# One more product on TensorE in bias steps 1 to 20 of an attention and mixture-of-experts kernel

## The chip, the core and the metric

The kernel runs on one core of one Trainium2 chip. The time is the device time of one execution in microseconds (us). The median of three runs of the kernel before is 584.39 us (584.32 to 586.5).

## What is computed

The reference does attention over 4 batches, 8 heads, 576 positions and a head size of 64, and then a top-1 mixture of 8 experts on its output. The part that matters here is the position bias that is added to the scores:

```python
psi_rel = np.log1p(np.abs(rel))
psi_i = np.log1p(np.maximum(pos[:, None].astype(np.float32), 1.0))
x = (psi_rel / psi_i)[..., None]
h = np.maximum(x @ w1 + b1, 0.0)      # hidden size 32
bias = h @ w2                         # one value for each head
scores = scores + bias.transpose(2, 0, 1)[None, :, :, :]
```

The bias is the same for all batches. Softmax, the product with v, the gate and the experts follow.

## The kernel before, in words

**Bias.** The bias of 576 rows is made in 36 steps of 16 rows (`bias_step`, `emit_hid`, `emit_bias`); a step takes 4 groups of 4 rows. For each group a hidden layer `hd` (128 partitions: 4 rows by 32 hidden units; up to 576 distances) is made from the table of log distances `tab` at line 196 on VectorE, or for the fourth group of some steps at line 194 on ScalarE. Eight such tiles exist. At line 210 TensorE multiplies each with the second-layer weights `w2blk` (32 columns) in fp32; the four products go to the partitions 0, 32, 64 and 96 of one PSUM tile `sps`, so each uses a strip of 32 of the array's 128 columns. An fp32 product shows as two matmuls in the trace. Steps have 304 to 576 distances; over 512 they need a second, narrow product. ScalarE moves the tile out in two pieces (lines 216 and 217, the first mirrored) and SyncE's queue writes it to memory (`bias_d`, line 219). After every eighth step a block of 128 rows is read back from memory in the layout of the scores (`load_bias`, lines 165 to 167).

**Numbering.** In the loop, `kk_done[0]` counts the steps. Iteration c makes the hidden layers of the c-th step and the products of the one before, so the products made in iteration 1 are those of the first 16 rows that are done; the text calls them step 1. Steps 1 to 16 have 448, 432, ... 304, 304, ... 384 distances, steps 17 to 21 have 576, 560, 544, 528 and 512. The first eleven iterations run ahead of the attention, the next eight two to each of the first four score units, then one to each unit.

**Scores.** A score unit (`emit_s`) puts two f16 matmuls into each half of a `sps` tile of the same pool: there are two such tiles, shared by score units and bias steps. VectorE adds the bias and takes the maximum (line 325), ScalarE the exponential (line 330). Transposes (lines 389, 405), their eviction (395, 406) and the product with v (417, 420) follow some units later. The first four score units need the first block of the bias, the next four the second.

**Order.** Up to the last score unit a planner orders the instructions of each engine by their place in the program and its own estimate of when each can run (only SyncE's queue follows the program's order in part of it); the order is fixed before the kernel starts. Loading and splitting of q, k and v for the first batches (lines 124, 147, 150) share the engines with the first bias steps.

Of the kernel before, what the change touches and what calls it, by code (L numbers as in the profile page):

```python
# [48 lines left out]
def build(tc, nc, io):  # L49
# [6 lines left out]
    def load_pack(name, fields):  # L56
        t = const.tile(list(io[name].shape), F32, name="c_" + name)
        nc.sync.dma_start(out=t, in_=io[name])
        views, o = [], 0
        for w in fields:  # L60
            views.append(t[:, o:o + w])
            o += w
        return views
# [32 lines left out]
    w1c, b1c, psi, ri8, w2blk = load_pack("cpa", CPA)  # L96
    tab = tab_p.tile([128, S], F32, name="tab")
# [84 lines left out]
    on128 = const.tile([128, 1], F32, name="on128")  # L182
    nc.vector.memset(on128, 1.0)

    def reach(kk):
        return max(16 * kk + 16, S - 16 * kk)

    def emit_hid(kk):
        n = reach(kk)
        for ct in range(4):  # L190
            k = 4 * kk + ct
            hd = hid_p.tile([128, S], F32, name="hd")
            if ct == 3 and kk_done[0] in HACT:
                nc.scalar.activation(out=hd[:, 0:n], in_=tab[:, 0:n], func=AF.Relu, bias=bp[:, k:k + 1])
            else:
                nc.vector.tensor_scalar(  # L196
                    out=hd[:, 0:n], in0=tab[:, 0:n], scalar1=bp[:, k:k + 1], scalar2=0.0,
                    op0=ALU.add, op1=ALU.max,
                )
            hid_t[k] = hd  # L200

    def emit_bias(kk):
        n = reach(kk)
        nb, nf = 16 * kk + 15, S - 16 * kk
        ps = s_ps.tile([128, 2, 512], F32, name="sps").rearrange("p a j -> p (a j)")
        for c0, c1 in ((0, min(n, 512)), (512, n)):
            if c0 >= c1:
                continue
            for ct in range(4):
                nc.tensor.matmul(  # L210
                    out=ps[32 * ct:32 * ct + 32, c0:c1], lhsT=w2blk, rhs=hid_t[4 * kk + ct][:, c0:c1],
                    start=True, stop=True,
                )
        bv = bev_p.tile([128, S + 15], F32, name="bv")
        sc = ri8[:, kk:kk + 1]
        nc.scalar.activation(out=bv[:, 0:nb], in_=ps[:, nb:0:-1], func=AF.Copy, scale=sc)
        nc.scalar.activation(out=bv[:, nb:nb + nf], in_=ps[:, 0:nf], func=AF.Copy, scale=sc)
        o = 16 * kk * H * BP + BPAD - 15
        wr_t[kk] = nc.sync.dma_start(
            out=bias_d[o:o + 16 * (H * BP + 1)].rearrange("(i c) -> i c", c=H * BP + 1)[:, 0:H * BP]  # L220
            .rearrange("i (h p) -> i h p", p=BP)[:, :, 0:S + 15],
            in_=bv,
        )
# [3 lines left out]
    kk_done = [0]  # L227
# [3 lines left out]
    def bias_step(n):  # L231
        for _ in range(n):
            c = kk_done[0]
            if c > NKK:
                return
            if c < NKK:
                emit_hid(KORD[c])
            if c:
                emit_bias(KORD[c - 1])
                if c % 8 == 0 or c == NKK:  # L240
                    load_bias(0, KORD[c - 1] // 8)
                if c in PC[1:]:
                    load_pair(PC.index(c), 0)
                if c in VC:
                    load_v(VC.index(c), 0)
            kk_done[0] += 1
# [883 lines left out]
    out = io["out"]  # L1130
# [76 lines left out]
    with fin:  # L1207
# [18 lines left out]
        for i in range(2):  # L1226
            nc.tensor.matmul(
                out=cn[:, i:i + 1], lhsT=amat16[:, i], rhs=R["cs"][:, S - 1:S], start=True, stop=True
            )
        nc.vector.tensor_scalar(  # L1230
            out=nbc.rearrange("p a k -> p (a k)"), in0=bcut[0:32], scalar1=cn[:, 0:1], scalar2=None, op0=ALU.is_lt
# [7 lines left out]
        for i in (2, 3):  # L1239
            nc.tensor.matmul(out=cn[:, 2 + i:3 + i], lhsT=amat[:, i], rhs=nb[:, 2:3], start=True, stop=True)  # L1240
        nc.vector.scalar_tensor_tensor(
            out=R["thh"], in0=nb[:, 1:2], scalar=128.0, in1=cn[:, 1:2], op0=ALU.mult, op1=ALU.subtract
        )
        nc.vector.scalar_tensor_tensor(
            out=gp[:, 1], in0=cn[:, 1:2].to_broadcast([32, B]), scalar=-1.0, in1=gmat, op0=ALU.add, op1=ALU.mult
# [5 lines left out]
            out=rbox["h16"][:, 0:S], in0=R["cs"], scalar=R["thh"], in1=es, op0=ALU.is_gt, op1=ALU.mult  # L1251
# [3 lines left out]
            out=ecm[:, K1:NF], in0=c128[0:8, 0:NF - K1], scalar1=cn[0:8, 3:4], scalar2=None, op0=ALU.is_ge  # L1255
        )
        nc.vector.tensor_scalar(
            out=ecm[:, NF:], in0=c128[0:8, 0:NH], scalar1=cn[0:8, 5:6], scalar2=None, op0=ALU.is_ge
        )
        nc.vector.tensor_scalar(  # L1260
            out=hsh, in0=cn[:, 4:5], scalar1=cn[:, 3:4], scalar2=128.0 * (NF - K1), op0=ALU.subtract, op1=ALU.add
# [10 lines left out]
            out=ez, in0=ecm.unsqueeze(2).to_broadcast([8, NBLK, NE]),  # L1272
# [11 lines left out]
        for b in range(K1, K1 + 2):  # L1284
# [4 lines left out]
            out=mkp.rearrange("p k e -> p (k e)"), lhsT=on[0:8, 0:128], rhs=ez.rearrange("p k e -> p (k e)"),  # L1289
            start=True, stop=True,  # L1290
        )
        for b in range(K1, K1 + 2):
# [6 lines left out]
            out=mk, in0=mkp, in1=emadd.unsqueeze(1).to_broadcast([128, NBLK, NE]), op=ALU.add  # L1299
# [18 lines left out]
        for i, m in enumerate((FSURE, HSURE)):  # L1318
            nc.vector.tensor_scalar(
                out=rest[:, i:i + 1], in0=emp[:, NBLK + i:NBLK + i + 1], scalar1=-float(m), scalar2=0.0,  # L1320
# [5 lines left out]
            out=i1, in0=sls, scalar1=0.0, scalar2=float(NT // 2 - 1), op0=ALU.is_lt, op1=ALU.add  # L1326
# [5 lines left out]
            out=odh, in0=i1[:, NF:NF + HSURE], scalar1=2.0, scalar2=hmask[:, 1:2], op0=ALU.mult, op1=ALU.add  # L1332
# [155 lines left out]
```

## Time and profile before

| | |
|---|---|
| median of 3 runs | 584.39 us |
| the profiled execution | 583.0 us |
| its span, first to last instruction | 581.2 us |
| mean granted TensorE clock | 0.977 |
| TensorE matmuls busy | 536.6 us (92%) |
| VectorE busy | 469.1 us (81%) |
| ScalarE busy | 436.8 us (75%) |
| GpSimd busy | 262.4 us (45%) |

The times of instructions come from one profiled execution, counted from its first instruction. A granted clock of 1.00 is 2.4 GHz, 0.50 is 1.2 GHz. The clock is on record from about 8.4 us on; what is shown as 1.00 ahead of that has no record.

### The profile page before, as it was taken

Reading aid. Unit: us, or ns where it says so; the run is one execution under the profiler, and the core shown is the slowest. Engines: PE = TensorE matmul, PEld = TensorE weight load, DVE = VectorE, ACT = ScalarE, POOL = GpSimd, SP = SyncE. Lnnn points to the kernel's source line nnn. Section 1 sums busy time; section 2 is a strip of 40 time slices with the busy share of each in tenths; the row PEclk is TensorE's granted clock in tenths of the full one; section 3 lists DMA queues with packets and bytes.
Section 4 is the critical chain, followed back from the end, with each engine's and each line's share of the span. In section 5 each row is a group of like instructions: output and inputs, shape, how many; then the busy total and the mean of one; then the engine's idle time right before and its main releaser. Section 6 shows DMA issues by size and latency. Waiting matters only on the chain. (4 is left out here: it accounts for less than half of the span.)

```text
span 581.2 us, 14263 instructions
## 1 busy us (share of the span) xinstructions
PE 536.6 (92%) x5319; PEld 361.3 (62%) x5319; DVE 469.1 (81%) x913; ACT 436.8 (75%) x743; POOL 262.4 (45%) x293
## 2 busy tenths in 40 slices
PE   4777999989999999999999998999999999999992
PEld 1233445755666666767577777667776877777851
DVE  7977886688889989887977558869999799797960
ACT  5877887866988877877689965568898687886940
POOL 5100000795199968966744760642424264323121
PEclk9888999999999999999999997998999999999997
DMA  8765447755798799745175010597899957988250
GB/s 287 247 181 157 135 132 211 258 174 144 176 256 209 194 280 232 205 103 163 49 257 147 3 34 13 129 342 239 280 204 368 262 120 236 199 211 230 25 184 30
DMA packets 99613, 106.15 MB, mean 183 GB/s; under 512 B 66893, under 2 KB 76239, under 8 KB 95442
## 3 DMA queue, kind: packets, MB, share of 16 engines
q1 hardware_dynamic: 94752, 89.45, 55.4%
q0 software_dynamic: 4640, 15.43, 9.7%
q8 instruction: 44, 0.72, 0.5%
q10 hardware_dynamic: 146, 0.30, 0.1%
q14 instruction: 31, 0.25, 0.1%
HBM read 128.92 MB, written 20.80 MB: 258 GB/s over the span
## 5 line engine op out<-in xcount | busy, mean ns | idle before, releaser
L330 ACT ACTIVATE e<-e,st 128x576 f32<-128x576 f32 x144 | 111.6, 776 | 12.1 <-DVE st L325 10.8
L325 DVE CUSTOM_DVE_ANT_0 e<-sps,wb 128x576 f32<-128x576 f32 x144 | 106.8, 750 | 16.0 <-PE sps L306 8.8
L905 DVE TENSOR_TENSOR w<-wb,w 128x2048 bf16<-128x2048 f32 (+1 forms) x36 | 72.4, 2050 | 2.2 <-ACT w L898 1.9
L1002 POOL DMA_INDIRECT out_dram<-y,odx x17 | 31.7, 1865 | 90.3 <-ACT y L992 53.4
L305 PE MATMUL sps<-kh,qs 128*128 128x288 f16 x256 | 68.9, 290 | 3.4 <-DVE st L325 1.7
L389 PE MATMUL ta<-c_cpb,e 128*128 128x128 f32 x448 | 71.2, 280 | 0.5 <-ACT eT L395 0.2
L395 ACT COPY eT<-ta 128x512 f32<-128x512 f32 x96 | 54.9, 581 | 21.9 <-PE ta L389 20.5
L306 PE MATMUL sps<-kl,qs 128*128 128x288 f16 x256 | 68.2, 288 | 0.0
L898 ACT CAST w<-wb 128x2048 f16<-128x2048 f32 (+1 forms) x40 | 63.8, 1640 | 3.4 <-DMA wb<-in_w_dram 3.4
L937 PE MATMUL sps<-xT,we 128*128 128x128 f16 (+1 forms) x1056 | 62.9, 222 | 3.0 <-DVE we L905 1.7
L937 PEld LDWEIGHTS <-we 128*128 128x128 f16 (+1 forms) x1056 | 61.4, 99 | 6.5 <-DVE we L905 1.9
L976 PE MATMUL yp<-w,hhT 128*128 128x512 bf16 (+1 forms) x272 | 64.3, 379 | 0.0
L420 PE MATMUL av<-eT,vt 128*64 128x320 f32 (+1 forms) x384 | 62.4, 424 | 0.0
L210 PE MATMUL sps<-hd,c_cpa 128*32 128x512 f32 (+17 forms) x352 | 46.3, 520 | 16.7 <-DVE hd L196 10.3
L389 PEld LDWEIGHTS ta<-c_cpb,e 128*128 128x128 f32 x448 | 52.3, 142 | 12.8 <-issue 2.7
L196 DVE TENSOR_SCALAR hd<-tab,bp 128x448 f32<-128x448 f32 (+17 forms) x129 | 49.9, 446 | 4.9 <-PE sps L210 4.8
L905 DVE TENSOR_TENSOR we<-ws,we 128x2048 bf16<-128x2048 f32 (+1 forms) x25 | 49.0, 1992 | 4.6 <-ACT we L898 3.3
L937 PEld LDWEIGHTS <-wb 128*128 128x128 f16 (+1 forms) x1056 | 49.6, 101 | 2.8 <-issue 1.2
L937 PE MATMUL sps<-xT,wb 128*128 128x128 f16 (+3 forms) x1056 | 51.3, 212 | 0.0
L898 ACT CAST we<-ws 128x2048 f16<-128x2048 f32 (+1 forms) x26 | 41.4, 1636 | 4.1 <-DMA ws<-in_w_dram 4.1
L420 PEld LDWEIGHTS av<-eT,vt 128*64 128x64 f32 x384 | 26.9, 136 | 26.5 <-issue 8.2
L976 PEld LDWEIGHTS <-hhT 128*128 128x128 f16 x272 | 25.8, 98 | 28.4 <-issue 0.3
(234 smaller groups left out, 1012.1 us busy)
## 6 DMA issues: line engine op xcount, KB each, us to landing
ws<-in_w_dram SPq DMA_DIRECT2D x34, 1024.0 KB
wb<-in_w_dram SPq DMA_DIRECT2D x34, 1024.0 KB
hs<-in_w_dram SPq DMA_DIRECT2D x20, 1024.0 KB
bias_d<-bv SPq DMA_DIRECT2D x36, 295.5 KB
kf<-in_kt_dram SPq DMA_DIRECT2D x24, 288.0 KB
wb<-bias_d SPq DMA_DIRECT2D x16, 288.0 KB
wb<-bias_d SPq DMA_DIRECT2D x16, 256.0 KB
xrow_d<-xo SPq DMA_DIRECT2D x16, 256.0 KB
```

The costliest lines, as they stand in the source:

```text
L196: nc.vector.tensor_scalar(out=hd[:, 0:n], in0=tab[:, 0:n], scalar1=bp[:, k:k + 1], scalar2=0.0, op0=ALU.add, op1=ALU.max,)
L305: nc.tensor.matmul(out=ps[:, half, 0:288], lhsT=lq, rhs=kh[:, j], start=True, stop=False)
L306: nc.tensor.matmul(out=ps[:, half, 0:288], lhsT=lq, rhs=kl[:, j], start=False, stop=True)
L325: nc.vector.tensor_tensor_reduce(out=e, in0=ps[:, :, 0:288], in1=bsl, scale=-0.125, scalar=1e30, op0=ALU.add, op1=ALU.min, accum_out=st[:, ...
L330: nc.scalar.activation(out=e, in_=e, func=AF.Exp, scale=-1.0, bias=st[:, 0:1], accum_out=sm)
L389: nc.tensor.transpose(out=ta[:, j, :], in_=e[:, o:o + 128], identity=ident)
L395: nc.scalar.copy(out=eTv[:, :, hh, o:o + 128], in_=ta)
L420: nc.tensor.matmul(out=av[64 * x:64 * x + 64, 0:n], lhsT=vt[:, j, 64 * x:64 * x + 64], rhs=eT[:, 2 * j + x, 0:n], start=False, stop=(j == 3),)
L898: nc.scalar.copy(out=wh[c][:, sl], in_=src)
L905: nc.vector.tensor_tensor(out=wl[c][:, sl], in0=src, in1=wh[c][:, sl], op=ALU.subtract)
L937: nc.tensor.matmul(out=hp.rearrange("p a j -> p (a j)")[:, n * f:n * f + n], lhsT=w[f // 4][:, o:o + 128], rhs=x[:, kt], start=(i == 0), s ...
L976: nc.tensor.matmul(out=yp, lhsT=x[:, kt], rhs=w[kt // 4][:, 512 * (kt % 4):512 * (kt % 4) + 512], start=(i == 0), stop=(i == len(terms) - 1),)
```

## The change

In iterations 1 to 20 one more fp32 product is put ahead of the step's own. Its weights are the same `w2blk`, its columns the first 384 of `tab`, and it goes to partitions 0 to 31 of the step's own PSUM tile, where the first of the four products then starts anew and overwrites it.

```diff
+    KEEP = range(1, 21)
+
     def reach(kk):
         return max(16 * kk + 16, S - 16 * kk)
...
         ps = s_ps.tile([128, 2, 512], F32, name="sps").rearrange("p a j -> p (a j)")
+        if kk_done[0] in KEEP:
+            nc.tensor.matmul(out=ps[0:32, 0:384], lhsT=w2blk, rhs=tab[:, 0:384], start=True, stop=True)
         for c0, c1 in ((0, min(n, 512)), (512, n)):
```

## Rows read from the trace of the kernel before

**Rows 1.** The page: busy time and share; the granted clock in 40 slices.

```profile
PE 536.6 (92%) x5319; PEld 361.3 (62%) x5319; DVE 469.1 (81%) x913; ACT 436.8 (75%) x743; POOL 262.4 (45%) x293
PEclk9888999999999999999999997998999999999997
```

**Rows 2.** Stretches: length; busy us of PE, PEld, DVE, ACT, POOL; clock; DMA share, GB/s.

```profile
8.36:25.43 17.07, 10.44 (x50) 2.96 (x48) 16.49 (x38) 14.74 (x30) 5.94 (x13) 1.00 0.90 301
25.43:28.84 3.41, 3.27 (x16) 0.85 (x16) 2.87 (x6) 2.39 (x7) 0.00 (x0) 0.50 0.32 127
28.84:35.67 6.83, 3.65 (x25) 1.25 (x23) 4.65 (x13) 3.96 (x10) 0.00 (x0) 1.00 0.86 235
35.67:39.08 3.41, 3.23 (x16) 1.33 (x15) 2.58 (x10) 2.20 (x6) 0.00 (x0) 0.50 0.54 153
39.08:52.74 13.66, 10.18 (x104) 4.95 (x103) 11.60 (x31) 11.23 (x27) 0.00 (x0) 1.00 0.61 173
52.74:56.15 3.41, 3.41 (x23) 1.73 (x24) 1.98 (x5) 2.07 (x6) 0.00 (x0) 0.50 0.32 105
56.15:120.00 63.85, 62.92 (x506) 34.87 (x505) 46.44 (x128) 49.75 (x114) 14.37 (x25) 1.00 0.63 185
```

**Rows 3.** TensorE in order of time: start, us, instructions, wait before them.

```profile
14.10 1.26 PE L210 MATMUL sps<-hd,c_cpa 128*32 128x416 f32 x4 [1.82 <-DVE hd L196]
...
23.53 1.27 PE L210 MATMUL sps<-hd,c_cpa 128*32 128x336 f32 x6 [2.03 <-DVE hd L196]
25.57 4.11 PE L210 MATMUL sps<-hd,c_cpa 128*32 128x336 f32 x18 [0.77 <-ACT hd L194]
...
31.13 1.47 PE L210 MATMUL sps<-hd,c_cpa 128*32 128x304 f32 x8 [0.86 <-DVE hd L196]
34.04 0.75 PE L210 MATMUL sps<-hd,c_cpa 128*32 128x320 f32 x8 [1.44 <-ACT bv L217]
35.85 0.40 PE L305 MATMUL sps<-kh,qs 128*128 128x288 f16 x1 [1.06 <-DVE st L325]
...
51.33 0.28 PE L305 MATMUL sps<-kh,qs 128*128 128x288 f16 x1 [1.11 <-ACT bv L217]
...
56.98 1.06 PE L210 MATMUL sps<-hd,c_cpa 128*32 128x512 f32 x8
```

**Rows 4.** TensorE's waits from 5 to 57 us: us in total, times, longest.

```profile
PE sps L210 <- DVE hd L196: 10.3, 5, 5.2
PE sps L210 <- ACT bv L217: 2.7, 4, 1.4
```

**Rows 5.** TensorE in order of time: steps 14, 17 with 18, 19, and 20.

```profile
39.18 0.80 PE L210 MATMUL sps<-hd,c_cpa 128*32 128x352 f32 x8
...
45.38 2.12 PE L210 MATMUL sps<-hd,c_cpa 128*32 128x512 f32 x32 [0.81 <-ACT bv L217]
...
49.10 1.13 PE L210 MATMUL sps<-hd,c_cpa 128*32 128x512 f32 x16 [0.24 <-ACT bv L217]
...
52.74 2.02 PE L210 MATMUL sps<-hd,c_cpa 128*32 128x512 f32 x16 [0.76 <-DVE st L325]
```

**Rows 6.** ScalarE: evictions of steps 8 and 13; VectorE: the first score tile.

```profile
26.94 0.47 ACT L216 ACTIVATE bv<-sps,c_cpa 128x255 f32<-128x255 f32 x1 [0.86 <-PE sps L210]
38.39 0.54 ACT L216 ACTIVATE bv<-sps,c_cpa 128x335 f32<-128x335 f32 x1 [1.21 <-PE sps L210]
35.03 0.76 DVE L325 CUSTOM_DVE_ANT_0 e<-sps,wb 128x576 f32<-128x576 f32 x1 [1.08 <-DMA wb<-bias_d]
```

**Rows 7.** SyncE's queue: bias writes and loads; VectorE: the fifth score tile.

```profile
27.87 3.39 SPq L219 DMA_DIRECT2D bias_d<-bv  x3
31.48 0.41 SPq L165 DMA_DIRECT2D wb<-bias_d  x1
45.35 2.80 SPq L219 DMA_DIRECT2D bias_d<-bv  x2
51.92 0.76 DVE L325 CUSTOM_DVE_ANT_0 e<-sps,wb 128x576 f32<-128x576 f32 x1 [0.39 <-DMA wb<-bias_d]
```

## Prediction

> **What bounds the kernel now.** I read the page's shares first: TensorE is busy for 92% of the span, VectorE and ScalarE for 81% and 75% [rows 1]. So time that TensorE loses in a stretch where its own queue is full is lost for good, and time that it waits for others is not its to lose. The granted clock by slice shows where it ran below full speed. Then I cut the first 57 us at the edges of the clock's falls [rows 2]: from 25.43, 35.67 and 52.74 us the clock stands at 0.50 (1.2 GHz) for 3.41 us each, and in those three stretches TensorE is busy for 3.27, 3.23 and 3.41 us, while in the stretches between it is busy for only 10.44 of 17.07, 3.65 of 6.83 and 10.18 of 13.66 us. The clock falls where the queue is full again, after a thin stretch: ahead of the first fall stand waits of 2.03 and 0.77 us, ahead of the second 1.44 us (and another 1.06 before 35.85), ahead of the third 1.11 and 0.76 us [rows 3]. The waits tell what makes the thin stretches: hidden layers that VectorE or ScalarE has not yet made, and the two score tiles in PSUM that are not yet free ("bv L217" is their eviction) [rows 4]. From 56.15 to 120 us TensorE is busy for 62.92 of 63.85 us [rows 2]. So the reader should carry one number through: when the products of step 21, the first without an extra, start. Now it is 56.98 us [rows 3], and what is gained or lost there mostly reaches the end.
>
> **The change, part by part.** It removes nothing and moves nothing; no DMA, VectorE, ScalarE or GpSimd instruction is added. The constant KEEP issues nothing. Added are 20 fp32 products (each two matmuls with their weight loads), all on strip 0 of the array's columns (32 of 128).
>
> *Price of one extra.* Two steps of 576 and 560 columns, back to back at full clock, take 2.12 us; one of 544 takes 1.13 us [rows 5]. The second of the two thus adds 0.99 us for some 592 columns, 1.67 ns a column for a whole fp32 product of two passes. The extra has 384 columns: 384 x 1.67 = 0.64 us of strip 0. At half clock a step of 528 columns takes 2.02 us against 1.13 [rows 5], a factor of 1.8 to 2 a column, so 1.2 to 1.3 us. An extra is worth between nothing (its strip would have waited) and 1.3 us; all 20 exposed at full clock would be 12.8 us. Its weight loads have 32 columns like the products' own and cost nothing of their own while a matmul runs (the weight loader is the lesser of the two busy times in every stretch [rows 2]).
>
> *Whom it delays.* A step's four products go to four strips. Eight matmuls of 352 columns take 0.80 us [rows 5]; one after the other they would take 8 x 352 x 0.83 = 2.3 us, so strips run side by side. An extra therefore delays strip 0 of its step, and the step's end only where strip 0 is the last to finish. The Trainium skill says it otherwise ("TensorE: Matmul & The Clock Gate", Part 3, The mechanism: matmuls start and end in strict program order). With each product's two passes in program order that would hold strips 1 to 3 behind the extra too; the 0.80 us speak against it. By the rule step 11 would also pay its 0.64 us, and the sum below would be -0.6 instead of -1.2 us.
>
> *The wait it adds.* The extra needs the step's PSUM tile free; the step's first product waited for that as well. Behind it in TensorE's queue stand the step's four products and then scores and transposes.
>
> *Steps 1 to 11 (to 32 us): nothing.* Their tile is free before their last hidden layer is there. The rows show TensorE waiting on hidden layers at 14.10, 23.53, 25.57 and 31.13 us [rows 3], 10.3 us on VectorE's in all (5.2 of it ahead of the first product) [rows 4] and some more on ScalarE's. Strip 0, whose layer comes first, has the gaps to itself. If that cover were gone, 11 x 0.64 = 7 us.
>
> *First fall.* Extras of steps 8 and 9 lie in or beside the waits ahead of it (2.03, 0.77 us). If the clock holds, the eviction of step 8, which waited 0.86 us for TensorE until 26.94 [rows 6], starts some 0.6 us earlier (the last product's two passes of 336 columns, 2 x 0.56 at half clock against 2 x 0.28). That eviction matters: its write, issued at 27.87, lets the bias load go at 31.48, and the first score tile waits for that load until 35.03 [rows 6, 7]. So 0.6 us earlier there.
>
> *Steps 12 to 14 and the second fall.* Step 12 waits for its tile until 34.04, so its extra is exposed: 0.64 us. It falls on the eviction, and ScalarE later waits 1.21 us for TensorE (until 38.39) [rows 6], which takes it up. In the second fall 3.23 us of work shrink to 1.6; the extras of 13 and 14 put 1.3 back. Net -0.3, on top of the 0.6, less a little for coupling: I keep -0.6 us at 41 us.
>
> *Steps 15 to 18 (41 to 49 us): nothing.* All four are exposed on TensorE, 2.6 us, but the fifth score tile, which follows step 18 directly (the steps 17 and 18 end at 45.38 + 2.12 = 47.50 [rows 5]), is not evicted until 51.92, for want of its bias load [rows 7]. That load hangs on the write at 45.35 [rows 7]. So TensorE may be some 4 us late here; ScalarE, which sets the write, works without a wait in the meantime. Without that cover: 2.6 us.
>
> *Steps 19, 20 and the third fall.* Step 19's extra pushes its eviction and the next scores (51.33) by 0.64, of which the 0.6 us of the earlier load and the wait of 0.76 before 52.74 take back about half: step 20 starts 0.3 us early. The 3.41 us of work in the third fall need 1.7 at full clock, plus 0.64 for step 20's extra: 2.35 against 3.41, so -1.05. Together -1.35; step 21 waits for step 20's eviction, which does not shorten, so I take -1.2 us at step 21.
>
> *What is late next.* From there TensorE is the bound to 120 us [rows 2] and the same order of work follows 1.2 us earlier. Against the profiled execution (583.0 us, a span of 581.2 with 1.8 around it) that gives 581.8. That execution lies 1.4 us below the median of the timed runs, 584.39; the same -1.2 there gives **583.2 us**.
>
> The order is written by a planner that sees 20 more matmuls, and I cannot read from these rows what it then does with scores and transposes; I allow 2 us either way for that, three times one extra.
>
> **Rivals.**
> 1. *The clock falls all the same, and the extras are paid at half speed (slower).* For it: an extra fills 0.64 us of thin stretches whose waits sum to 2 to 3 us each [rows 3], and in two of them it waits for the same tile as the products, so it fills nothing until the tile comes. Against: a wait of 1.82 us before 14.10 did not bring the clock down [rows 2, 3], so waits about as long as these can pass. Place: step 13, in the second fall, at half clock costs 1.3 us, step 14 0.64; ScalarE's wait of 1.21 takes up the first part, so the write at 45.35 and the load behind it go 1.1 us later. Step 20 adds 1.3 at half clock. Sum +2.4 us: **586.8 us**. It decides from the second fall on: if 0.50 is still granted after 35 us, the sign turns. With steps 15 to 19 uncovered as well, +3.2: 590.
> 2. *The extras are all hidden, the clock holds (more gain).* Half of 3.27 + 3.23 + 3.41 = 5.0 us comes back, less only the extras of 13, 14 and 20 where these find another wait: -3 to -5, **580.4 us**. For it: waits of 10 us in the stretch. Against: from 33 us on the extra stands behind the same wait as the products.
> 3. *No change.* The clock holds but the score tiles go on waiting for bias loads whose time is set by VectorE's hidden layers and the DMA, and TensorE gets back in falls what it spends in extras: **584.4 us**. For it: the loads' round trips of 6.6 to 7.2 us [rows 7] have no TensorE in them.
>
> **How the numbers follow.** Chances: the forecast 0.40, rival 1 0.25, rival 2 0.13, rival 3 0.22. The forecast's own range is 581.2 to 585.2 (2 us either way for the planner). For 8 in 10 I reach to rival 2's 580.4 and to 587.8, past rival 1 by 1 us. A measurement of this kernel can tell some 0.5% (2.9 us) from no change: faster means under 581.5, slower over 587.3. Faster: nearly all of rival 2 and a fifth of the forecast (its low end), 0.20. Slower: some four tenths of rival 1, a tenth of the others for the planner, with steps 15 to 19 in it, 0.20. The rest, 0.60, is within.
>
> **What would show it.** Right: 1.00 granted from 9 to 120 us; the eviction of step 8 at about 26.3; the first score tile evicted at about 34.4, the fifth at 51.3; step 21 at about 55.8, with nothing changed behind it but the shift. Steps 1 to 11 wrong if VectorE shows waits on TensorE's products before 28 us. Wrong in the mechanism if 0.50 still stands after 35 or 52 us; wrong in the sum if step 21 moves and the end does not, or if matmuls, scores and transposes stand in another order on TensorE.

## The result, and the profile after

The changed kernel takes 589.45 us (median of 6 runs, 585.13 to 593.28), the kernel before on the same chip 583.27: a ratio of 1.0113 [1.0071, 1.0154]. On another chip it was 587.21 against 583.83, 1.0047 [1.0016, 1.0078]. The forecast was 583.2. The profiled execution of the changed kernel took 593.28 us, the longest of its six, against 583.0 for that of before; so its single times are read with care below, and the second profile of the changed kernel stands beside it where they differ. Line numbers behind line 205 are 4 higher than before: the extra is line 209, the products 214, the evictions 220 and 221, the score tile 329, the DMA transposes 354, the product that reads them 364.

The clock did what the forecast said. The page's first lines (answering to [rows 1]): no early slice is under 9 tenths.

```profile
PE 545.5 (92%) x5342; PEld 366.3 (62%) x5359; DVE 467.1 (79%) x913; ACT 437.6 (74%) x743; POOL 263.1 (44%) x293
PEclk9999999989989998999999997998999999999997
```

The stretches of [rows 2] in the changed kernel, and two later ones: 1.00 to 120 us. In the three stretches that ran at half clock before, TensorE is now busy for less of the time (2.51, 2.85 and 3.13 us against 3.27, 3.23 and 3.41), and from 56 to 120 us for as much as before. Behind 120 us it is busy for less of the time, at 0.94 and 0.97.

```profile
25.43:28.84 3.41, 2.51 (x20) 0.89 (x20) 3.04 (x7) 3.10 (x8) 0.00 (x0) 1.00 0.41 145
35.67:39.08 3.41, 2.85 (x22) 1.36 (x25) 1.84 (x8) 3.26 (x8) 0.00 (x0) 1.00 0.24 72
52.74:56.15 3.41, 3.13 (x28) 1.65 (x28) 2.39 (x7) 2.89 (x7) 0.00 (x0) 1.00 0.49 144
56.15:120.00 63.85, 62.84 (x508) 35.01 (x507) 46.80 (x130) 49.80 (x114) 14.68 (x25) 1.00 0.65 191
120.00:150.00 30.00, 26.65 (x201) 17.84 (x202) 25.81 (x62) 20.11 (x46) 17.18 (x20) 0.94 0.56 137
150.00:270.00 120.00, 111.73 (x922) 75.60 (x920) 96.11 (x247) 94.06 (x215) 88.40 (x98) 0.97 0.80 194
```

The same two late stretches of the kernel before (120 to 150, 150 to 270 us):

```profile
120.00:150.00 30.00, 27.20 (x221) 18.12 (x221) 26.86 (x67) 21.75 (x49) 17.66 (x20) 1.00 0.60 150
150.00:270.00 120.00, 114.94 (x981) 79.26 (x977) 102.72 (x261) 99.44 (x230) 92.39 (x103) 1.00 0.78 205
```

The rows of single instructions in the changed kernel that answer to [rows 3, 6, 7]: the products of step 8 that wait for ScalarE's hidden layer and their eviction, the extra of step 20 beside its products, step 21, and the first, fifth and ninth score tile.

```profile
26.15 1.29 PE L214 MATMUL sps<-hd,c_cpa 128*32 128x336 f32 x10 [0.45 <-ACT hd L196]
26.94 0.47 ACT L220 ACTIVATE bv<-sps,c_cpa 128x255 f32<-128x255 f32 x1 [0.28 <-PE sps L214]
54.37 0.51 PE L209 MATMUL sps<-tab,c_cpa 128*32 128x384 f32 x1
54.39 0.63 PE L214 MATMUL sps<-hd,c_cpa 128*32 128x512 f32 x3
54.72 0.49 PE L209 MATMUL sps<-tab,c_cpa 128*32 128x384 f32 x1
57.28 1.07 PE L214 MATMUL sps<-hd,c_cpa 128*32 128x512 f32 x8
35.02 0.76 DVE L329 CUSTOM_DVE_ANT_0 e<-sps,wb 128x576 f32<-128x576 f32 x1 [1.34 <-DMA wb<-bias_d]
51.86 0.76 DVE L329 CUSTOM_DVE_ANT_0 e<-sps,wb 128x576 f32<-128x576 f32 x1 [1.30 <-PE sps L214]
61.17 0.76 DVE L329 CUSTOM_DVE_ANT_0 e<-sps,wb 128x576 f32<-128x576 f32 x1
```

TensorE's waits from 5 to 57 us, answering to [rows 4] (us in total, times, longest): what was a wait of the products for VectorE's hidden layers is now one of the extras for their tile and, ahead of the first, for the table.

```profile
PE sps L209 <- DVE tab L99: 4.9, 1, 4.9
PE sps L209 <- ACT bv L221: 4.6, 7, 1.4
PE sps L214 <- DVE hd L198: 1.2, 2, 0.7
```

Up to the score tile at 97.4 us the two profiles are level (61.17 against 61.01, 97.44 against 97.43). Then the changed kernel falls behind: 1.7 us at score tile 36 of 144, 4.6 at 60, 8.3 at 100, 9.6 at 140, 10.2 at the last block of the experts. The order of instructions on every engine is that of before from 65 us on. TensorE's waits from 140 to 270 us show what is new; first the changed kernel, then the kernel before (us in total, times, longest):

```profile
PE av L364 <- DMA eT<-e: 6.5, 6, 1.9
PE av L421 <- DVE eT L410: 1.0, 3, 0.5
```

```profile
PE av L417 <- DVE eT L406: 2.1, 3, 0.8
PE av L416 <- DVE xt L373: 1.6, 3, 0.7
PE tb_r L403 <- DVE eT L406: 0.9, 2, 0.6
```

eT is the transposed e in f16 that two DMA transposes bring to each of eight groups in the middle ("pieces" below); the kernel before never waits for one. Such waits in TensorE's order of time in the changed kernel:

```profile
151.88 0.38 PE L364 MATMUL av<-eT,v 128*128 128x256 f16 x2 [0.74 <-DMA eT<-e]
170.79 0.38 PE L364 MATMUL av<-eT,v 128*128 128x256 f16 x2 [1.51 <-DMA eT<-e]
222.29 0.28 PE L364 MATMUL av<-eT,v 128*128 128x256 f16 x1 [1.94 <-DMA eT<-e]
```

Another part of this profile's loss is three clock falls of 3.41 us at 123.6, 171.4 and 222.6 us, each behind such a wait or, the first, behind one of 2.57 us for VectorE. The second profile of the changed kernel has the waits (5.3 us) and none of these falls, so the waits are what the two have in common. They are no measure of the loss by themselves: as the rows show, waits for VectorE shrink beside them (4.6 us in the three rows of before, 1.0 in the one of the changed kernel).

### The profile page after: what moved, and what is told of

It reads as the page before. It is cut to its first block, busy times and chain, and to the rows that moved or that the text cites. A ratio compares the mean times of both kernels' runs of the same rounds, so it can differ in the third digit from the quotient of the medians.

```text
span 591.4 us, 14321 instructions
## 1 busy us (share of the span) xinstructions
PE 545.5 (92%) x5342; PEld 366.3 (62%) x5359; DVE 467.1 (79%) x913; ACT 437.6 (74%) x743; POOL 263.1 (44%) x293
## 5 line engine op out<-in xcount | busy, mean ns | idle before, releaser
L980 PE MATMUL yp<-w,hhT 128*128 128x512 f16 (+1 forms) x255 | 63.2, 379 | 2.3 <-ACT w L902 1.4
L214 PE MATMUL sps<-hd,c_cpa 128*32 128x512 f32 (+17 forms) x352 | 48.7, 482 | 2.6 <-DVE hd L198 1.2
```

The source lines that it names most:

```text
L980: nc.tensor.matmul(out=yp, lhsT=x[:, kt], rhs=w[kt // 4][:, 512 * (kt % 4):512 * (kt % 4) + 512], start=(i == 0), stop=(i == len(terms) - 1),)
```

## The experiments

Each was timed in 12 runs (the pair with plain copies in 6) beside 17 to 35 of the kernel before on the same chip. A ratio with an interval that holds 1 can't be told from no change.

**The kernel before again** (no edit).

> The kernel before, unchanged, as a second profile and a control. Chance theory (the 1.1% come from executions that differ from one to the next, in DMA landings and clock falls after 110 us): ratio to before within 0.3%, but the profile shows falls of the clock in other places than 25, 36, 53, 353 and 394 us, and some of them between 110 and 300 us as in the kernel after. Order theory and cost theory: ratio 1.000, falls at 25, 36 and 53 us again, none between 60 and 340 us.

0.9989 [0.9953, 1.0025]; the clock fell at 25.0 and 35.2 us again, TensorE did not wait for eT.

**The changed kernel again** (no edit).

> The kernel after, unchanged. Chance theory: anywhere from 0.995 to 1.012. Order theory and cost theory: 1.011 again, the clock at 1.00 up to 110 us, and the loss again after 110 us (units 32 to 120 of the score tiles late by 5 to 10 us, while unit 28 is within 1 us of the kernel before).

1.0047 [1.0016, 1.0078]: slower, by less than at first. No fall before 371 us, and six waits for eT:

```profile
PE av L364 <- DMA eT<-e: 5.3, 6, 1.2
```

**The extras in two parts.** `KEEP = range(1, 12)` leaves them in steps 1 to 11, `range(12, 21)` in steps 12 to 20. The first has the order of instructions of the kernel before, the second that of the changed kernel.

> KEEP is range(1, 12): only the extras ahead of the attention; every engine's order of the other instructions is that of the kernel before. Cost theory as predicted (these extras are hidden): time of before, -0.6 us at most, ratio 0.999 to 1.000. Order theory: 1.000, since the order is that of before. Theory that a clock held early is paid for later (any held clock moves falls to the middle): 1.005 or more.

0.9973 [0.9935, 1.001]; no early clock fall, and the ninth score tile at 58.75 us.

> KEEP is range(12, 21): only the extras beside the attention; every engine's order of the other instructions is that of the kernel after. Order theory: 1.011, all of the loss. Cost theory: 9 extras of 0.64 us, some 2.6 us of them covered, 1.003 to 1.005, visible already at 60 us. Chance theory: between 0.995 and 1.012.

1.0003 [0.9971, 1.0034]; clock falls at 16.1, 26.3 and 36.6 us, the ninth score tile at 62.46. Neither the early extras, nor the late ones with the planner's new order, cost what both cost together. So the loss is not a sum of the extras' prices, and it is not the order, as far as these intervals tell. The waits for eT were 0.7 and 0.4 us.

**What else 20 products change.** They are 80 TensorE instructions (an fp32 product shows as two matmuls and two weight loads). The page of both kernels counts transfers of instructions during the run; here the changed kernel's:

```profile
q8 instruction: 44, 0.72, 0.5%
```

That is 16 KB each. Put beside the instructions that TensorE had begun, one comes for every 254 of them on average (single distances go from some 100 to 400), so 80 more move them by about a third of their distance against the program. In the three kernels below with 256 instructions more the page counts one transfer more; that of the changed kernel with 44 products of one column:

```profile
q8 instruction: 45, 0.74, 0.5%
```

So the transfers follow the number of TensorE's instructions. Each piece waits for its second transpose. From the issue of that transpose to the start of the first piece, the DMA of the changed kernel (144.50 to 151.88 us) carries one of these transfers; that of the kernel before (142.87 to 149.30) shows no line for them:

```profile
DMA packets 3606, 1.67 MB, mean 227 GB/s; under 512 B 2704, under 2 KB 3275, under 8 KB 3605
q1 hardware_dynamic: 3605, 1.66, 95.9%
q8 instruction: 1, 0.02, 1.0%
```

```profile
DMA packets 3603, 1.64 MB, mean 255 GB/s; under 512 B 2707, under 2 KB 3281, under 8 KB 3603
q1 hardware_dynamic: 3603, 1.64, 113.4%
```

To move the transfers and nothing else, products of one column were put ahead of the first step, where TensorE waits 5.2 us [rows 4]; four TensorE instructions each, and the order of all else stays:

```diff
+    for _ in range(20):
+        nc.tensor.matmul(out=tb_r[0:32, 0:1], lhsT=on[:, 0:32], rhs=on[:, 0:1], start=True, stop=True)
     NKK = NG // 4
```

**The kernel before with 20 of them**: as many instructions as the extras.

> The kernel before with 20 fp32 products of one column ahead of the first bias step, into a PSUM tile that later work overwrites: as many TensorE instructions as the 20 extras add (20 x 2 matmuls and 20 x 2 weight loads), at a time when TensorE has nothing to do; the order of all else is that of before. Theory A (instruction fetch): the page shows 44 transfers of 16 KB on the queue of kind instruction; by the instructions that TensorE had begun, they come every 256 of them, and each one in the changed kernel that stood beside the DMA transposes of e (landings near 150, 170, 183, 220, 250, 266 us) came with a wait of TensorE for eT. The 80 more instructions move these fetches against the program, so this kernel is slower like the changed one though it has none of its cost: ratio 1.004 to 1.010, 3 to 6 us of waits at the product of v and eT (line 364 of the changed kernel), as before three clock falls ahead of 60 us. Rival B (the cost or the order of the extras makes the loss): ratio 1.000, no such waits.

1.0062 [1.0032, 1.0092], as theory A had it. Two things were expected wrongly: the waits are longer than 3 to 6 us, and the early falls did not stay: this profile has none. Its waits for eT and its first piece:

```profile
PE av L362 <- DMA eT<-e: 7.5, 6, 2.2
148.67 0.38 PE L362 MATMUL av<-eT,v 128*128 128x256 f16 x2 [1.79 <-DMA eT<-e]
```

**The changed kernel with 44**: 176 and 80 make 256, one whole transfer.

> The changed kernel with 44 more fp32 products of one column ahead of the first bias step: 176 more TensorE instructions, 256 with those of the extras, which is one whole fetch. Theory A: the fetches stand against the middle of the program as in the kernel before; the waits of TensorE for the DMA transposes eT (5.3 and 6.5 us in the two profiles of the changed kernel) are gone but for at most 1 us, and with the clock held early the kernel is as fast as the one with extras in steps 1 to 11 alone: ratio 0.995 to 1.000. Rival B: nothing is mended, ratio 1.004 to 1.011 and the waits stay.

1.000 [0.9969, 1.0032], the upper end of theory A's range, and the waits are gone:

```profile
PE av L366 <- DMA eT<-e: 0.4, 2, 0.2
```

**The kernel before with 64** (256 instructions) **and with 32** (128).

> The kernel before with 64 fp32 products of one column ahead of the first bias step: 256 TensorE instructions, one whole fetch. Theory A: the fetches come at the same places of the program as before, so the ratio is 0.998 to 1.002 and TensorE waits under 1 us for eT. Rival C (more instructions as such, the length of the stream, cost the time): slower than the kernel with 20 tiny products, 1.010 or more. Rival B: 1.000 as well, so it is told from A by the kernel with 20.

0.999 [0.9957, 1.0023], 0.4 us of waits. Three times as many instructions as the 20 cost nothing, so it is not the length of the stream.

> The kernel before with 32 fp32 products of one column ahead of the first bias step: 128 TensorE instructions, half a fetch. Theory A: it depends on which instructions the fetches now stand at; those moved by 36 and 44 cost nothing, those by 80 (the changed kernel) 0.5 to 1.1%; by 128 the fetches come about 50 instructions ahead of where the changed kernel had them, so most of them miss the transposes' landings again: 0.998 to 1.006, with 0 to 3 us of waits for eT. Rival B: 1.000. Rival C: between the kernels with 20 and 64.

0.9979 [0.9951, 1.0007]: no loss in time, just under the range of theory A, though the waits are just over its 3 us:

```profile
PE av L362 <- DMA eT<-e: 3.1, 4, 1.2
```

**The pieces later**: `LCD = 6` for `LCD = 5`, in the changed kernel and in the kernel before.

> The changed kernel with the products of v and the transposed e (the pieces at line 364) one score unit, some 2.3 us, later: the constant LCD is 6 instead of 5, nothing else. The fetches still fall on the transposes, but TensorE now comes to the pieces some 2 us after the latest landing. Theory A (the loss is TensorE's wait for transposes that land late beside a fetch): the waits for eT go from 5.3 and 6.5 us to under 1.5, and the time goes to that of the same edit on the kernel before, within 0.3%. Rival D (the fetch costs TensorE itself time, the landing only shows it): TensorE waits elsewhere for as long, and the ratio stays 0.5% or more above that of the same edit on the kernel before.

> The kernel before with the same edit (LCD 6 instead of 5), the control for the run ahead of it: it has no waits for eT to lose, so 0.997 to 1.004, by what the later pieces do to the rest.

1.009 [1.0055, 1.0125] with 7.3 us of waits for eT, against 1.0009 [0.9976, 1.0042] with 0.9. The edit did not do what I meant: the planner left the pieces within a few instructions of where they stood (the first one did not move) and changed the order around them. So it does not test a later piece. It does show the loss of 0.8% again between kernels that differ in the extras alone, in another order of the middle.

**The kernel before with 48** (192 instructions).

> The kernel before with 48 fp32 products of one column ahead of the first bias step, 192 TensorE instructions. Theory A: with 128 the fetches still stood in the transposes' time (3.1 us of waits for eT); with 192 each comes another 64 instructions, some 3 us, earlier against the program, ahead of the second transpose of each pair: under 1.5 us of waits, ratio 0.996 to 1.001. If more instructions as such made the loss, it would be at or above the kernel with 20 (1.006).

1.0007 [0.9974, 1.0039] and 0.6 us of waits, as expected.

**Extras 1 to 11 with 53** (44 and 212 make 256).

> A candidate for faster than both: extras in bias steps 1 to 11 alone (0.9973 [0.9935, 1.001] in its own run) and 53 fp32 products of one column ahead of the first bias step, so that the TensorE instructions added are 44 + 212 = 256, one whole fetch. Theory A: waits for eT at most 0.5 us (0.7 with the extras alone), score tiles some 2 us earlier from the eighth on as with the extras alone, ratio 0.994 to 0.999. Rival B, which takes the early cost alone for the cause: the same as with the extras alone, 0.997.

1.0029 [0.9999, 1.0059]: the candidate is not faster, against the expectation. Its profile, of an execution of 590.88 us where the median is 584.98, is used below for its clock alone.

**Plain copies for the transposes**, in both kernels; the transposition is left out, and the bytes are moved all the same:

```diff
-            out=eT[:, :, QOFF[qt]:QOFF[qt] + 128], in_=e16.rearrange("p t j -> p (t j)"), transpose=True
+            out=eT[:, :, QOFF[qt]:QOFF[qt] + 128], in_=e16.rearrange("p t (k i) -> p (t k) i", i=128)
```

> The kernel before with the 16 DMA transposes of e replaced by plain copies of the same bytes from and to the same tiles (the transposition is left out, so the attention of these groups is not the reference's). Control for the next run. Each pair of transposes took 6 to 9 us to issue and land; plain copies should land well before TensorE comes to the pieces, so no waits for eT; time within 1% of before, either way, for the planner orders the middle anew.

> The changed kernel with the same replacement, in the same order of work as the run ahead of it but for the first 60 us. Theory A (the whole loss is the wait for transposes that land late beside an instruction fetch): with nothing to land late, no waits for eT and within 0.25% of the run ahead of it. Rival D (the fetch, the stream's length or the extras cost TensorE time also without the transposes): 0.5 to 1.1% slower than the run ahead of it, as the changed kernel is against the kernel before.

1.011 [1.0062, 1.0158] and 1.0145 [1.01, 1.019]. Neither waits for eT. The second is 0.35% above the first, between the two expectations, and the intervals overlap: this pair decides nothing. The first was expected within 1% of the kernel before and is just outside: the new order has other waits, 4.8 us of them for VectorE's score tiles from 100 to 350 us.

**Extras 1 to 11 once more.**

> The extras in steps 1 to 11 alone, once more. If what was seen (0.9973 [0.9935, 1.001], score tiles 2 us earlier from the eighth on) is the gain of a clock that is held early, 0.995 to 0.999 again; if it was a difference between executions, 1.000 to 1.003, like the run with 53 tiny products beside them (1.0029).

0.9997 [0.9963, 1.003], with no fall before 119.8 us, the ninth score tile at 58.36 us, and this time

```profile
PE av L364 <- DMA eT<-e: 4.0, 3, 1.7
```

The ratio lies between the two expectations (up to 0.999, from 1.000). The early gain is there again, and waits for eT with it, in the same kernel that had 0.7 us of them before.

**Side by side.** The run labelled as the changed kernel's third was by my mistake the kernel before, unedited; its expectation is therefore void, and it is one more control. The other two are what their texts say.

> The changed kernel once more, to stand beside the next two on the same chip: 1.004 to 1.011, 5 to 7 us of waits for eT.

1.0004 [0.9967, 1.004] (the kernel before), no waits for eT, clock falls at 25.8 and 36.0 us.

> The kernel before with 20 tiny products again (80 TensorE instructions, as many as the extras). Theory A: all of the changed kernel's loss is in the fetches, so it is as slow as the changed kernel, within 0.3%, at 1.004 to 1.009. Rival E (the fetches are a part, the cost of the extras in steps 12 to 20 another): 1.002 to 1.006, and 0.3% or more under the changed kernel.

1.0102 [1.0061, 1.0143], over theory A's range of 1.004 to 1.009; rival E had it at 1.002 to 1.006:

```profile
PE av L362 <- DMA eT<-e: 6.5, 6, 1.4
```

> The changed kernel with 28 tiny products, 112 TensorE instructions, so that 192 are added as in the run of the kernel before with 48 tiny ones (0.6 us of waits for eT there). Theory A: waits for eT under 1.5 us and 0.997 to 1.002. Rival E: the waits go as well, but 1.002 to 1.006 is left for the extras. Rival B: as the changed kernel, 1.004 to 1.011.

1.0022 [0.9993, 1.0051], just over the edge of theory A's range and just inside that of rival E, so a small price of the extras themselves is not excluded; the waits are

```profile
PE av L366 <- DMA eT<-e: 0.5, 2, 0.3
```

**All together.** Instructions added to TensorE's stream ahead of the middle; pieces of eight with an instruction transfer between the issue of their second transpose and their start; TensorE's waits for eT in the profile; the length of the middle, from the start of the 29th score tile to that of the last (144th); ratio. A star stands for each 3.41 us at half clock in the middle.

```
 added  kernel                      pieces  waits us  middle us          ratio
     0  before (profile, 2 again)   0 0 0   0  0  0   221.0 221.8 220.8  0.9989, 1.0004
    36  extras 12 to 20             4       0.4       222.3              1.0003
    44  extras 1 to 11 (twice)      4 4     0.7 4.0   221.9 225.1*       0.9973, 0.9997
    80  changed (twice)             7 6     6.5 5.3   231.3*** 224.4     1.0113, 1.0047
    80  before + 20 tiny (twice)    6 6     7.5 6.5   226.1 225.5        1.0062, 1.0102
   128  before + 32 tiny            3       3.1       223.2              0.9979
   192  before + 48 tiny            0       0.6       220.3              1.0007
   192  changed + 28 tiny           0       0.5       221.9              1.0022
   256  changed + 44 tiny           0       0.4       223.7*             1.0000
   256  before + 64 tiny            0       0.4       223.1*             0.9990
```

Every kernel with 80 instructions more is slower, and no other in this table is, whether its extras do work or not. Left out are the runs in another order of the middle and the one with 53 tiny products (256 instructions more, 1.0029). In three of the four profiles with 80 more the second piece waits without being counted: a transfer began 0.3 to 0.4 us ahead of the issue.

**Landing late, or no next instruction?** A wait for eT could also hide that TensorE lacked its next instruction while the transfer ran. The traces settle this: the end of a DMA is told by 16 updates of a semaphore, and they are on record. For the first, third, fifth and last piece of the changed kernel the last update comes at 151.84, 185.76, 222.25 and 268.22 us, 1.0 to 1.2 us behind the end of the transfer, and the piece starts at 151.88, 185.80, 222.29 and 268.27. In the first piece the other 15 updates are there by 150.38; in the kernel before all 16 come by 149.04. In every profile of the table each piece that waited started 0.04 or 0.05 us behind the last update. So the landing itself is reported late, and TensorE has its instruction.

## Why the prediction was wrong

*The step that failed* is the carry-through: "From there TensorE is the bound to 120 us [rows 2] and the same order of work follows 1.2 us earlier". The order did follow, but not at the same time: the instructions were cost as work and not as places in a stream. 80 of them moved the transfers of TensorE's own code into the time of the DMA transposes, these land late, and TensorE, the bound, waits 6.5 and 5.3 us for them in the two profiles; the middle is 10.1 and 3.2 us longer than before, where the forecast had nothing. The forecast's allowance of 2 us for the order of the planner was for another thing; its rivals had none for this, and "nothing changed behind it but the shift" was wrong. That the place in the stream decides is shown, by the 20 tiny products that make the loss and by the 44 and 28 that mend it. That the waits for eT are all of the loss is not: the pair with plain copies left it open, and 3.1 us of waits in the kernel with 32 showed no loss (its middle starts 2.0 us earlier than the mean of before and is 1.9 us longer).

*The clock: right, with one exception.* In eight profiles of kernels with extras in steps 1 to 11 the clock did not fall before 119 us; in three of the kernel before it fell two or three times ahead of 60 us. The exception is the run with 53 tiny products beside extras 1 to 11, in the execution that is not read otherwise: falls at 36.3 and 60.2 us. The timed runs agree in the mean: the granted clock is 0.984 to 0.987 in the kernels with all extras, 0.979 to 0.981 in the kernel before beside them. But a held clock does not need the extras: without them, the first profile with 20 tiny products has no early fall, and three others (20 again, 32, the later pieces) have one. Rival 1 (the clock falls all the same) does not explain the loss; it has its place in the first 57 us, where the changed kernel is level.

*Steps 1 to 11: right in the sum, not in the reason.* The extras there were to find their tile free; they wait for it, 2.9 us in five waits up to 32 us (the other two of the seven waits shown are those of steps 12 and 17), in time in which the products had waited for hidden layers. Alone they cost nothing.

*Price of an extra: right.* The extra of step 20 shows as two passes, 0.35 us apart (54.37 and 54.72), so some 0.7 for both; the forecast was 0.64. (It divided 0.99 us by some 592 columns; the step in its row has 560, which gives 0.68.) The step's other products start at 54.39, beside it. The Trainium skill's rule weighed in the forecast ("TensorE: Matmul & The Clock Gate", Part 3, The mechanism: starts in strict program order) would have held them behind both passes, if the two stand next to each other in the stream, which the trace does not show; on that condition the trace does not agree.

*The first fall's 0.6 us: wrong.* The eviction of step 8 starts at 26.94 as before [rows 6], not at 26.3. Its last product still waits for a hidden layer of ScalarE's, and TensorE goes on at 26.15 instead of 25.57 [rows 3]: what the full clock gives back, 0.6 us, the later layer takes. The first score tile stays at 35.02, the fifth at 51.86 [rows 6, 7].

*The sum at step 21: 57.28 in place of 55.8* against 56.98 [rows 3], so +0.3 and not -1.2. But one profile of before was a thin base: its other two have the ninth score tile at 62.69 and 62.66 (61.01 in the first), for which the clock gives no reason: their second fall lasted 6.8 us and not 3.41, but they had no third, so 10.2 us ran at half clock ahead of 60 us in all three. The mean of the three is 62.1; of the changed kernel and its two mended forms (61.17, 60.77, 60.90, 61.10) it is 61.0. That is 1.1 us earlier, the forecast's size, though not by its rows, and no more than a hint: with 20 to 64 tiny products and no extras the same tile stands anywhere from 59.15 to 63.05. The parts, too, are of the size that it thought of: extras 1 to 11 alone stand at 58.75 and 58.36, 3.5 us earlier, and extras 12 to 20 on top of them cost 2.4.

*The sum, profile by profile.* Against the mean of the three profiles of before, the middle of the changed kernel starts 1.6 us earlier in its first profile and 2.0 in its second, takes 10.1 and 3.2 us more, and what follows it takes 0.9 and 1.5 us more (there the three of before differ by up to 3.3 among themselves). Together that is 9.3 and 2.6 us, the differences of the spans. In the first profile 10.24 us of the middle ran at half clock, two thirds of it behind waits for eT. In the second, 5.3 us of such waits make only 3.2 us, because other waits shrink: TensorE stands idle in the middle for 11.8 us, against 9.2 in the mean of before. With 20 tiny products the two profiled executions (585.18 and 584.61 us) are among the fastest of their 12, whose medians are 588.94 and 589.69; what the longer ones add is in no profile, and clock falls behind the waits, as in the first profile of the changed kernel, are only a guess.

*Rival 3 (no change)* is what is left when the middle is mended: 1.000 and 1.0022. The early gain of 1 to 2 us (0.2 to 0.3%) is under what these intervals show. No version was found that is clearly faster than the kernel before; extras in steps 1 to 11 come nearest (0.9973 and 0.9997).

## What to carry to other kernels

Instructions that cost no time where they stand can cost time later, because they move every instruction behind them in the engine's stream: if a change that should be free, or hidden, makes a far stretch slower whose order has not changed, look at the instruction transfers there (in the profile's list of DMA queues), and put a number of one-column products that fills up a whole transfer beside the change before judging it. Compare the waits of the bound engine row by row between profiles: here one row that the kernel before did not have told the place. For its cost take the engine's whole idle time in that stretch, since other waits shrink beside a new one. And take early times from more than one execution of the kernel before, when the clock falls in them differ.

## What the runs showed of the hardware

- TensorE's instructions are transferred while the kernel runs: 44 times 16 KB, one for every 254 instructions begun on average (some 64 bytes each), each taking about 1 us; 45 times with 256 instructions more.
- Such a transfer beside DMA transposes delays their landing. When it started within 0.25 us of the last packet of the transposes, on either side, mostly one of the 16 updates of their semaphore came 1.0 to 1.2 us after the transfer's end, and the piece started 0.04 us later, 1.07 to 1.24 us after that end (149.60 to 150.76, start 151.88; 220.00 to 221.20, start 222.29; and the same in the kernel before with 20 tiny products: 146.39 to 147.55, start 148.67); in the first profile of extras 1 to 11 one that started 0.03 us behind the last of these packets, at 146.48, delayed nothing. When it came in the midst of them, twenty 256-byte packets took 1.8 to 2.6 us instead of a mean of 0.02 (at 166 us in the changed kernel), and the last update came 7.1 us after the issue where before it took 4.7.
- With 36 and 44 instructions more, a transfer fell into that time at four pieces of eight too, and the waits ranged from 0.4 to 4.0 us: such a transfer does not always cost. It costs nothing where the piece starts later than the landing all the same.
- The kernel before is near that edge: in its profile a transfer comes 0.9 us after the first piece has started (149.30, 150.20).
